# Attention followed by a mixture of experts: expert weights in quarters between the loads, q and k loaded pair by pair

## The chip, the core and the metric

The kernel runs on one core of a Trainium2 chip. The metric is the device time in microseconds of one execution; before the change it was 235.57 us, the median of three runs (233.94 to 238.21).

The engines are named as the profile names them: PE (TensorE, matrix products), DVE (VectorE), ACT (ScalarE), POOL (GpSimd), SP (SyncE, which only issues transfers here). Each runs its own instruction list strictly in order and waits on semaphores for the others. Transfers are issued by SP, ACT or POOL and are carried by 16 DMA engines that all of them share.

## The reference

```python
scores = scale * np.matmul(q, k.transpose(0, 1, 3, 2))    # (4, 8, 768, 768), head_dim 64
# retrieval heads 0, 2 and 6 see all earlier positions; the five streaming heads see the
# first 4 positions and a window of 64
mask = np.where(retr[0, :, 0, 0, None, None], full_mask, stream_mask)
a = softmax(np.where(mask, scores, -1e9));  attn = np.matmul(a, v)
x = attn.transpose(0, 2, 1, 3).reshape(3072, 512)
xc = x[x @ w_skip > 0];  logits = xc @ w_gate             # (512, 8)
e_idx = np.argmax(logits, axis=1);  gate_w = softmax(logits)[e_idx]
for e in range(8):
    h = np.maximum(xc[e_idx == e] @ w1[e], 0.0)           # (512, 1024)
    y[e_idx == e] = gate_w * (h @ w2[e])                  # (1024, 512)
out = x;  out[x @ w_skip > 0] = xc + y
```

So: attention for 4 x 8 heads of 768 tokens, then for the tokens with a positive skip score one expert of eight. The eight experts have two weight matrices each, 2 MB a matrix in fp32.

## The kernel before, in words

**Attention** goes over 16 pairs of heads (pair i: batch i // 4, heads 2(i % 4) and the next one). For each pair POOL casts q, k and v to fp16 (lines 659 and 665), PE transposes them (684, 695), ACT and DVE copy the transposes out of PSUM (`out_q` 712, `out_k` 722 with 729 and 730 for the sliding-window keys `kx`), PE forms the scores with their masks (818, 830), ACT takes the exponentials (840), PE weighs the values (881), and DVE divides (900, 907) and writes the pair's part of x (917). Three pairs in four have one retrieval head and one streaming head, the fourth has two streaming heads. For streaming heads POOL copies a part of the values (765, 767).

**Loads.** q, k and v of batch 0 come in parts, those of batches 1 to 3 as whole batches of 1.5 MB (`load`, 610 to 620), into five buffers that later also hold weights. For batch 0 a partition holds six tokens that follow each other, so a head's run is 1,536 bytes; for v and for the later batches a partition holds every 128th token, and a run is 256 bytes. SP issues them in order, together with the finished x of each batch (`x_out`, 926), which goes to `out`.

**Weights.** There are 16 halves (an expert's w1 or w2, 2 MB read, cast to 1 MB of fp16 on the way), numbered W0 to W15. POOL issues them (452), each at a place in its list tied to a cast. W0 to W10 stand in the attention part; W11 and W12 stand ahead of the gathers, W13 to W15 among and behind them.

**Routing** (1023 to 1057, then `fin`, 1122 to 1125): DVE and PE turn the gate logits into `idx`, 16 lists of 128 token rows, two lists for each expert.

**Experts.** POOL gathers the 16 lists of rows from `out` (1154), which must wait until all of x has been written there. For each list DVE casts (1178), PE transposes (1187), DVE copies out (1198). PE forms h for an expert (1207), ACT takes the relu (1218), PE forms y (1228), DVE adds gate times y to the rows (1235), and POOL scatters them back to `out` (1164). W0 and W1 belong to expert 0, W14 and W15 to expert 7.

**What sets the order.** Class `Plan` holds every step with an engine, an assumed duration, what it depends on and a priority. `lay` walks through time: it takes the engine that can start soonest and lets it do, of the steps that are ready there, the one with the lowest key. A transfer (`dma`) is two steps: the issue on an engine, and the transfer itself on a modelled queue "Q". `write` then emits the instructions in the order that came out. The order is fixed when the program is built: on the chip only semaphores decide when a step starts. There are two plans, one for attention with routing, one for the experts.

Of the kernel before, what the change touches and what calls it, by code (L numbers as in the profile page):

```python
# [52 lines left out]
class Plan:  # L53
# [8 lines left out]
    def op(self, name, eng, dur, fn, deps=(), key=0.0, lat=None, take=None):  # L62

        o = dict(name=name, eng=eng, dur=dur, fn=fn, deps=list(deps), key=key,
                 lat=self.LAT if lat is None else lat, take=take,
                 seq=len(self.ops))
        self.ops.append(o)
        self.by[name] = o
        return name

    def dma(self, name, eng, issue, kbytes, fn, deps=(), key=0.0, queue="Q",
            rate=370.0, lat=1.9):
        self.op((name, "go"), eng, issue, fn, deps, key)
        self.op(name, queue, kbytes / rate, None, [(name, "go")], len(self.ops),
                lat=lat)

    def lay(self, rings):
# [9 lines left out]
        ready, free, n = {}, {}, 0  # L87
# [5 lines left out]
        def at(o):  # L93
            if o["take"]:
                s = slots[o["take"][0]]
                if not s:
                    return None
                return max(when[o["name"]], min(s))
            return when[o["name"]]

        while n < len(self.ops):
# [21 lines left out]
            for u in users.get(o["name"], ()):  # L123
# [4 lines left out]
                if not need[u]:  # L128
                    ready.setdefault(v["eng"], []).append(v)
        return sorted(self.ops, key=lambda o: (o["start"], o["seq"]))  # L130

    def write(self, **rings):
        for o in self.lay(rings):
            if o["fn"] is not None:
                o["fn"]()

# [242 lines left out]
def kernel(  # L379
# [60 lines left out]
    NPRE = 7  # L440
    wts = {}

    def wtile(n, pool):
        e, half = divmod(n, 2)
        wts[e, half] = pool.tile([P, DS * F], FP16, name=f"w{half + 1}_{e}")
# [4 lines left out]
    def load_half(n):  # L450
        e, half = divmod(n, 2)
        nc.gpsimd.dma_start(out=wts[e, half], in_=(w1r, w2r)[half][e])

    ld_pool = ctx.enter_context(tc.tile_pool(name="ld", bufs=1))

    def slab(shape, dt, name):
        return ld_pool.tile(shape, dt, tag="big", bufs=5, name=name)

    def load_slab(n):
        def go():  # L460
            wts[divmod(n, 2)] = slab([P, DS * F], FP16, f"ws{n}")
            load_half(n)
        return go

    with tc.tile_pool(name="qk", bufs=1) as qk_pool, \
# [103 lines left out]
        dma("wgl", "ACT", 0.9, 60, l_wg, key=-90)  # L569
# [38 lines left out]
        big = {}  # L608

        def load(w, b, h0, h1, eng):  # L610
            def go():
                if h0 == 0:
                    big[w, b] = slab([P, H * NQB, D], FP32, w + "f")
                t = big[w, b][:, h0 * NQB:h1 * NQB]
                if b == 0 and w != "v":
                    eng.dma_start(
                        out=t.rearrange("p (h n) d -> p h (n d)", n=NQB),
                        in_=rows6[w][b, :, h0:h1])
                else:
                    eng.dma_start(out=t, in_=rows1[w][b, :, h0 * NQB:h1 * NQB])  # L620
            return go

        sp = iter(range(1000))
        where = {}
        order = [("q", 0, 0), ("k", 0, 0), ("v", 0, 0), ("q", 0, 1), ("k", 0, 1),
                 ("v", 0, 1), ("q", 0, 2), ("k", 0, 2), ("q", 0, 3), ("k", 0, 3)]
        order += [(w, b, 0) for b in range(1, B) for w in "qkv"]
        slabs = []
        for w, b, n in order:
            hs = (0, H) if b else (2 * n, 2 * n + 2)  # L630
            if (w, b, n) == ("v", 0, 1):
                hs = (2, H)
            for i in range(4 * b + hs[0] // 2, 4 * b + hs[1] // 2):
                where[w, i] = ("ld", w, b, n)
            old = None
            if n == 0:
                slabs.append((w, b))
                if len(slabs) > 5:
                    w2, b2 = slabs[-6]
                    old = ("C" + w2, 4 * b2 + 3)  # L640
            on_act = (w, b, n) == ("k", 0, 0)
            dma(("ld", w, b, n), "ACT" if on_act else "SP", 0.45,
                197 * (hs[1] - hs[0]) * (1.25 if w == "v" and not n + b else 1.06),
                load(w, b, *hs, nc.scalar if on_act else nc.sync),
                [old] + ([("ld", "q", 2, 0)] if w + str(b) == "k2" else []),
                -95 if on_act else next(sp))


        def fp32_of(w, i):
            h0 = 2 * (i % 4)  # L650
            return big[w, i // 4][:, h0 * NQB:(h0 + 2) * NQB].rearrange(
# [18 lines left out]
        for i in range(NPR):  # L670
            for w in "qk":
                op(("C" + w, i), "DVE" if i == 0 and w == "q" else "POOL", 0.87,
                   cast(i, w), [where[w, i], ("T" + w, i - 2)],
                   10 * (i - 2) + (1 if w == "q" else 2))
            op(("Cv", i), "POOL", 0.9, cast_v(i),
               [where["v", i], ("PV", i - 3, 1), ("Vx", i - 3), "vones"],
# [24 lines left out]
        def in_order(i, to, t):  # L701

            if i < 4:
                return (to.rearrange("d (p n) -> d p n", n=NQB),
                        t.rearrange("d n p -> d p n"))
# [639 lines left out]
```

## Time and profile before

| | us |
|---|---|
| median of three runs (233.94 to 238.21) | 235.57 |
| the execution that was profiled | 236.37 |
| its span, first to last instruction | 234.8 |
| attention and routing, to the last of `idx` and its gates | 0 to 134.84 |
| from there to the first gather | 134.84 to 151.91 |
| first product of an expert to the last | 159.18 to 221.73 |
| from there to the end of the span | 13.1 |

The profile is of one execution. A row of the view by line gives engine, operation, tiles, the shape, the count, the busy time, the mean of one in ns, and the idle time of the engine ahead of them with what ended it. The view by stretches gives the busy time of each engine in a stretch, then the clock of TensorE that was granted (1.00 is full), the busy share of the 16 DMA engines, and the GB/s they moved. "Busy" of an engine leaves out its waits; an idle engine costs time only where another waits for it.

### The profile page before, as it was taken

What the parts mean: (1) busy time and instruction counts of PE and PEld (TensorE: products, weight loads), DVE (VectorE), ACT (ScalarE), POOL (GpSimd) and SP (SyncE); (2) the same over time, 40 slices, a digit from 0 to 9 for tenths busy, and PEclk for the clock granted to TensorE, in tenths of its full rate; (3) what the DMA queues carried; (4) which work ended last, traced back from release to release, by engine and by line L of the source; (5) the groups of instructions that cost most, each with busy time, mean ns of one, the idle gap of its engine ahead of it and who ended that gap; (6) DMA issues with size and microseconds to landing.
All of it is one profiled execution on the core that took longest, in us unless ns stands there. A gap on an engine that the chain in (4) does not pass through costs nothing. (4 is left out here: it accounts for less than half of the span.)

```text
span 234.8 us, 4538 instructions
## 1 busy us (share of the span) xinstructions
PE 156.6 (67%) x1817; PEld 122.4 (52%) x1832; DVE 114.8 (49%) x305; ACT 98.3 (42%) x119; POOL 103.5 (44%) x158
## 2 busy tenths in 40 slices
PE   0597877893588953988872400019889999999700
PEld 0375666773477742877751300018756887667300
DVE  6576584752355732369999900035318645312400
ACT  2167465884077760688565900003143442234000
POOL 7639347900939207963361000177874233122510
PEclk9999799999589996799998555557999999999985
DMA  6999999998999999999999999236499931101100
GB/s 178 341 345 275 260 299 296 254 283 216 305 368 298 229 245 290 250 194 185 259 252 242 227 245 262 52 86 183 91 201 229 211 143 46 46 11 51 48 25 1
DMA packets 29517, 47.09 MB, mean 201 GB/s; under 512 B 4644, under 2 KB 23972, under 8 KB 27442
## 3 DMA queue, kind: packets, MB, share of 16 engines
q0 software_dynamic: 4864, 21.55, 42.4%
q1 hardware_dynamic: 23296, 24.77, 33.6%
q10 hardware_dynamic: 1330, 0.41, 0.7%
q8 instruction: 16, 0.26, 0.4%
q14 instruction: 11, 0.09, 0.1%
HBM read 56.64 MB, written 10.49 MB: 286 GB/s over the span
## 5 line engine op out<-in xcount | busy, mean ns | idle before, releaser
L840 ACT ACTIVATE at<-pst 128x1024 f16<-128x1024 f32 (+1 forms) x60 | 58.2, 1007 | 42.0 <-PE pst L830 41.5
L1218 ACT ACTIVATE ht<-hps 128x512 f16<-128x512 f32 x32 | 19.1, 597 | 61.7 <-PE hps L1207 52.9
L830 PE MATMUL pst<-qT,k 128*128 128x128 f16 (+2 forms) x308 | 38.0, 251 | 5.9 <-ACT qT L712 3.3
L830 PEld LDWEIGHTS <-k 128*128 128x128 f16 x308 | 26.1, 105 | 16.5 <-issue 8.1
L1164 POOL DMA_INDIRECT out_dram<-xg,idx x16 | 16.1, 1003 | 32.4 <-DVE xg L1235 29.9
L722 DVE COPY k<-tps 64x768 f16<-64x768 f16 x32 | 20.9, 654 | 16.0 <-PE tps L684 15.7
L881 PEld LDWEIGHTS <-at 128*128 128x128 f16 x472 | 19.2, 100 | 15.9 <-issue 12.0
L659 POOL CAST k<-kf 128x768 f16<-128x768 f32 x16 | 13.2, 825 | 30.5 <-DMA kf<-in_k_dram 29.7
L1154 POOL DMA_INDIRECT xg<-out_dram,idx x16 | 16.9, 1055 | 16.7 <-DMA out_dram<-x 12.1
L881 PE MATMUL opsa<-va,at 128*128 128x74 f16 x392 | 21.4, 199 | 3.5 <-DVE x L917 3.5
L1207 PE MATMUL hps<-xT,w 128*128 128x256 f16 x192 | 23.4, 281 | 0.2 <-issue 0.2
L1187 PE MATMUL xtp<-ident,x 128*128 128x128 f16 x64 | 6.4, 241 | 24.9 <-DVE x L1178 24.3
L1207 PEld LDWEIGHTS <-w 128*128 128x128 f16 x192 | 21.9, 145 | 1.5 <-issue 0.4
L1235 DVE SCALAR_TENSOR_TENSOR xg<-yps,gsl,xg 128x512 f32<-128x512 f32 x16 | 11.9, 749 | 18.3 <-PE yps L1228 17.9
L1178 DVE CAST x<-xg 128x512 f16<-128x512 f32 x16 | 9.5, 626 | 23.2 <-DMA xg<-out_dram,idx 23.2
L1228 PEld LDWEIGHTS <-ht 128*128 128x128 f16 x128 | 12.3, 98 | 14.0 <-issue 0.5
L1187 PEld LDWEIGHTS <-x 128*128 128x128 f16 x64 | 4.7, 107 | 26.1 <-DVE x L1178 25.1
L1228 PE MATMUL yps<-w,ht 128*128 128x512 f16 x80 | 18.1, 379 | 0.4 <-issue 0.4
L818 PE MATMUL pst<-smask,identb 128*128 128x512 bf16 (+3 forms) x49 | 16.9, 358 | 0.0
L665 POOL CAST va<-vf 128x768 f16<-128x768 f32 x16 | 13.1, 825 | 8.1 <-DMA vf<-in_v_dram 6.9
L881 PE MATMUL opsa<-vx,at 128*128 128x74 f16 x80 | 8.8, 207 | 11.7 <-POOL vx L767 11.7
L765 POOL COPY vx<-va 64x296 f16<-64x296 f16 x20 | 9.9, 493 | 14.7 <-DVE va L754 5.7
(120 smaller groups left out, 263.6 us busy)
## 6 DMA issues: line engine op xcount, KB each, us to landing
w<-in_moe_w_dram POOLq DMA_DIRECT2D x11, 1024.0 KB
ws<-in_moe_w_dram POOLq DMA_DIRECT2D x5, 1024.0 KB
out_dram<-x SPq DMA_DIRECT2D x3, 1536.0 KB, 18.6
qf<-in_q_dram SPq DMA_DIRECT2D x4, 384.0 KB, 5.3
kf<-in_k_dram SPq DMA_DIRECT2D x3, 384.0 KB, 5.0
out_dram<-x SPq DMA_DIRECT2D x1, 768.0 KB, 23.0
out_dram<-x SPq DMA_DIRECT2D x2, 384.0 KB, 20.4
kf<-in_k_dram ACTq DMA_DIRECT2D x1, 384.0 KB, 4.7
```

The costliest lines, as they stand in the source:

```text
L659: e.tensor_copy(t, fp32_of(w, i).rearrange("p h n d -> p n h d"))
L665: nc.gpsimd.tensor_copy(vab[i % 3][:, :, GX:GX + 2 * D].rearrange("p n (h d) -> p h n d", h=2), fp32_of("v", i))
L722: nc.vector.tensor_copy(to, ti)
L818: nc.tensor.matmul(pst[:, c0 - c * CH:c0 - c * CH + m].rearrange("p (n c) -> p n c", c=P), identb, mv, start=(n == 0), stop=(n == last))
L830: nc.tensor.matmul(pst[:, c0 - c * CH:c0 - c * CH + m * P], lt, qTs[i][:, qb * P:(qb + m) * P], start=(n == 0), stop=(n == last))
L840: nc.scalar.activation(ats[i][:, c * CH:c * CH + cn], psts[i, c][:, :cn], ACT.Exp, scale=SCALE)
L881: nc.tensor.matmul(opss[i][:, hi, qb * VA:(qb + 1) * VA], ats[i][:, b0 + c:b0 + c + P], vb, start=(n == 0), stop=(n == len(todo) - 1))
L1154: h = nc.gpsimd.indirect_dma_start(out=xgs[:, t], out_offset=None, in_=out[:, :], in_offset=bass.IndirectOffsetOnAxis(ap=idx[:, t:t + 1], ...
L1164: h = nc.gpsimd.indirect_dma_start(out=out[:, :], out_offset=bass.IndirectOffsetOnAxis(ap=idx[:, t:t + 1], axis=0), in_=xgs[:, t], in_offs ...
L1207: nc.tensor.matmul(hps[:, fi, :], w1[:, s, 2 * f2 + fi], xTs[e][:, s, :], start=(fi == 0 and s == 0), stop=(fi == 1 and s == DS - 1))
L1218: nc.scalar.activation(hts[e][:, 2 * f2:2 * f2 + 2], hpss[e, f2], ACT.Relu)
L1228: nc.tensor.matmul(yps, hts[e][:, j, s2 * P:(s2 + 1) * P], w2[:, j], start=(j == 0), stop=(j == FS - 1))
```

## The change

It changes how the weights are cut and where their issues stand, how q and k are loaded, and a few steps of routing:

- Weights go in quarters (half of a W, 1 MB read). In the plan each quarter has `fill`: its issue may not start before the modelled queue has less than that many us left to do (0.5 in attention, 2.0 for the experts). Quarters have the last priority in attention. Those that the plan would start after `idx` are left to the second plan, where they alternate with the gathers.
- q and k are loaded pair by pair, all with six tokens to a partition, into four buffers each (`load_qk`); v stays in batches, in two buffers. `out_q` and `out_k` then have the reordering copy for all pairs that batch 0 had before, and the `kx` copies read the copied k instead of PSUM.
- x of a batch is written in two transfers instead of one.
- Routing: the token lists' table `R` is made by POOL instead of DVE; the one-hot table `L` in 4 operations over six columns each instead of 24 over one.
- A drain stands on POOL behind the twelfth scatter.
- The modelled durations are adjusted.

```diff
-    def lay(self, rings):
+    def lay(self, rings, busy=0.0):
...
         def at(o):
+            t = when[o["name"]]
+            if o["fill"] is not None:
+                more = sum(x["dur"] for x in ready.get("Q", ()))
+                t = max(t, free["Q"] + more - o["fill"])
...
-        nc.gpsimd.dma_start(out=wts[e, half], in_=(w1r, w2r)[half][e])
+        c = slice(u * DS * F // 2, (u + 1) * DS * F // 2)
+        def go():
+            nc.gpsimd.dma_start(out=wts[e, half][:, c],
+                                in_=(w1r, w2r)[half][e][:, c])
...
+        def load_qk(i, w, eng):
+            def go():
+                b, hs = heads(i)
+                t = ldq_pool.tile([P, 2, NQB, D], FP32, tag=w + "f", bufs=NLD,
+                                  name=w + "f")
+                eng.dma_start(out=t.rearrange("p h n d -> p h (n d)"),
+                              in_=rows6[w][b, :, hs[0]:hs[0] + 2])
...
-            if i < 4:
-                return (to.rearrange("d (p n) -> d p n", n=NQB),
-                        t.rearrange("d n p -> d p n"))
-            return to, t.rearrange("d n p -> d (n p)")
+            return (to.rearrange("d (p n) -> d p n", n=NQB),
+                    t.rearrange("d n p -> d p n"))
...
-            dma(("W", n), "POOL", 0.9, 2097,
-                load_slab(n) if n >= NPRE else lambda n=n: load_half(n),
-                [after] + free, 10 * after[1] - 15.5, rate=400)
+            dma(name, "POOL", 0.58, 2.65, load_quarter(*name[1:]),
+                [("Cv", 1), (fill[x - 1], "go") if x else None], 500 + x,
+                first=True, fill=0.5)
...
-                "R": lambda: v.tensor_tensor(
+                "R": lambda: nc.gpsimd.tensor_tensor(
...
-                fns["L", m] = lambda m=m: v.tensor_scalar(
-                    T["L"][:, c0 + m], iota16, h128[:, m:m + 1],
-                    rank[:, m:m + 1], ALU.add, ALU.is_equal)
+                fns["L", m] = lambda m=m: v.tensor_tensor(
+                    T["L"][:, c0 + m:c0 + m + NQB], ...
...
+            dma(name, "POOL", 0.58, 2.65, load_quarter(*name[1:]),
+                [(fill[x - 1], "go") if x else None], -50 + x, first=True,
+                fill=2.0)
+        for t in range(NT):
+            dma(("G", t), "POOL", 1.25, 0.4, gather(t), [("z", t // 2 * 2)],
+                -100 + t if t < 4 else -48 + 0.7 * t, first=True)
...
+        op("drain", "POOL", 2.0, lambda: nc.gpsimd.drain(), [("S", 11)], 11.5)
```

How the order moves. POOL, the start of the program, after the change; `ident` is the identity for the transposes, `w_3_95` holds W7, expert 3's w2:

```order
L516 MEMSET ident 128x128
L474 DMA w_3_95<-in_moe_w_dram 128x2048
L517 ISA
L517 AFFINE_SELECT ident<-ident 128x128
L523 CAST identb<-ident 128x128
```

Before, no transfer stood there, and W0 was the first weight, behind the casts of the third pair. Now one quarter of W7 (the second plan's first) comes out at the very start, and W0's first quarter stands behind the casts of k of the eighth pair. Up to the gathers there are 16 quarters, W0 to W7, instead of 13 halves.

POOL around the end of attention, before (`ws` and `w` are weights, `vx` the copied values of streaming heads, `xg` the gathered rows):

```order
L452 DMA ws_2064<-in_moe_w_dram 128x4096
L765 COPY vx_131<-va_127 64x296
L767 COPY vx_131<-va_127 64x296
L452 DMA ws_2150<-in_moe_w_dram 128x4096
L452 DMA w_5_2305<-in_moe_w_dram 128x4096
L452 DMA w_6_2306<-in_moe_w_dram 128x4096
L1154 DMA xg<-out_dram,idx 128x512 x12
L452 DMA w_6_2307<-in_moe_w_dram 128x4096
L1154 DMA xg<-out_dram,idx 128x512 x4
```

and after the change:

```order
L779 COPY vx_136<-va_132 64x296
L781 COPY vx_136<-va_132 64x296
L1065 TENSOR_TENSOR tables<-r_oht,val 128x18x64
L474 DMA w_3_94<-in_moe_w_dram 128x2048 x2
L474 DMA w_3_95<-in_moe_w_dram 128x2048
L1065 TENSOR_TENSOR tables<-r_oht,val 128x6x64
L1174 DMA xg<-out_dram,idx 128x512 x4
L474 DMA w_4_96<-in_moe_w_dram 128x2048
L1174 DMA xg<-out_dram,idx 128x512
L474 DMA w_4_96<-in_moe_w_dram 128x2048
L1174 DMA xg<-out_dram,idx 128x512 x3
L474 DMA w_4_2346<-in_moe_w_dram 128x2048
```

Before, W10, W11 and W12 stood between the last copy of values and the first gather, each a half. Now three quarters stand there (W6 whole, the first of W7) beside the two steps that make `R`, and W8 to W10 alternate with the gathers. W11 to W15 follow in quarters among the first ten scatters.

## Rows read from the trace of the kernel before

**Rows 1.** The page: span; DMA's busy tenths in 40 slices of 5.87 us.

```profile
span 234.8 us, 4538 instructions
DMA  6999999998999999999999999236499931101100
```

**Rows 2.** By stretches: busy (x count) PE, PEld, DVE, ACT, POOL; clock, DMA share, GB/s.

```profile
50.00:100.00 50.00, 34.81 (x493) 28.95 (x497) 22.59 (x60) 25.90 (x30) 24.79 (x41) 0.86 1.00 274
100.00:135.00 35.00, 23.84 (x393) 19.52 (x395) 31.44 (x104) 25.31 (x29) 12.62 (x22) 0.90 1.03 226
135.00:152.00 17.00, 0.00 (x0) 0.00 (x0) 0.00 (x0) 0.00 (x0) 0.62 (x2) 0.50 0.81 193
159.00:222.00 63.00, 61.04 (x442) 44.62 (x440) 25.72 (x54) 19.06 (x32) 28.10 (x29) 0.98 0.45 113
```

**Rows 3.** Waits: who waited for whom, us in total, times, the longest.

```profile
POOL k L659 <- DMA kf<-in_k_dram: 29.7, 4, 11.7
```

**Rows 4.** POOL in order of time: start, us, the instruction, idle before it.

```profile
46.04 0.53 POOL L452 DMA_DIRECT2D w<-in_moe_w_dram  x1
...
58.28 0.83 POOL L659 CAST k<-kf 128x768 f16<-128x768 f32 x1 [11.72 <-DMA kf<-in_k_dram]
```

**Rows 5.** DVE in order of time: x of pairs 4, 6, 8, 10, 12, 14.

```profile
50.37 0.95 DVE L917 TENSOR_TENSOR x<-opsa,recs 128x768 f32<-128x768 f32 x1
...
69.12 0.94 DVE L917 TENSOR_TENSOR x<-opsa,recs 128x768 f32<-128x768 f32 x1
...
80.88 0.94 DVE L917 TENSOR_TENSOR x<-opsa,recs 128x768 f32<-128x768 f32 x1
...
99.98 0.94 DVE L917 TENSOR_TENSOR x<-opsa,recs 128x768 f32<-128x768 f32 x1
...
112.11 0.95 DVE L917 TENSOR_TENSOR x<-opsa,recs 128x768 f32<-128x768 f32 x1
...
124.50 0.94 DVE L917 TENSOR_TENSOR x<-opsa,recs 128x768 f32<-128x768 f32 x1
```

**Rows 6.** DMA queues, whole span: packets, MB written, share of 16 engines' time.

```profile
q0 software_dynamic: 4864, 21.55, 42.4%
q1 hardware_dynamic: 23296, 24.77, 33.6%
```

**Rows 7.** The same from 100 to 135 us (q0 POOL's, q1 SP's).

```profile
q0 software_dynamic: 829, 6.04, 87.3%
q1 hardware_dynamic: 1022, 1.81, 14.6%
```

**Rows 8.** In order of time: routing's end, first gather, its cast, expert products.

```profile
134.66 0.18 DVE L1125 TENSOR_TENSOR gsl<-msb 128x16 f32<-128x16 f32 x1
...
151.91 1.10 POOL L1154 DMA_INDIRECT xg<-out_dram,idx  x1 [12.08 <-DMA out_dram<-x]
155.31 1.15 DVE L1178 CAST x<-xg 128x512 f16<-128x512 f32 x2 [20.47 <-DMA xg<-out_dram,idx]
159.18 1.91 PE L1207 MATMUL hps<-xT,w 128*128 128x256 f16 x8
218.11 3.62 PE L1228 MATMUL yps<-ws,ht 128*128 128x512 f16 x16
```

**Rows 9.** By tile x: its transfers to out, from issue to landing.

```profile
DMA to landing us min/median/max: 11.8/20.8/31.5
```

**Rows 10.** DVE: one line's durations in ns; then groups by line.

```profile
L722 DVE COPY k<-tps x32: 538/560/961, 10.7 to 115.0; 64x768 f16<-64x768 f16 x32
L729 DVE COPY kx<-k 64x256 f16<-64x256 f16 x5 | 2.4, 487 | 0.2
L729 DVE COPY kx<-tps 64x256 f16<-64x256 f16 x15 | 4.3, 284 | 0.0
L1057 DVE TENSOR_SCALAR tables<-iota,r_h,r_rank 128x128 f16<-128x128 f16 x24 | 6.1, 325 | 0.0
```

**Rows 11.** SP's waits at the program's end.

```profile
SPq L1340 <- PEq L1340: 6.7, 2, 6.2
```

More of the change, by code (lines that the diff above doesn't have):

```diff
@@ L69, in op, with dma @@
         return name
[L71 to L74, printed above, removed]
+    def dma(self, name, eng, issue, took, fn, deps=(), key=0.0, first=False,
+            lat=1.9, fill=None):
+        self.op((name, "go"), eng, issue, fn, deps, key, fill=fill)
+        self.op(name, "Q", took, None, [(name, "go")], 0 if first else 1,
                 lat=lat)
-    def lay(self, rings):
+    def lay(self, rings, busy=0.0):
         users, need, gives = {}, {}, {}
@@ L86, in lay @@
         when = {o["name"]: 0.0 for o in self.ops}
[L87 removed]
+        ready, free, n = {}, {"Q": busy}, 0
         slots = {r: [0.0] * m for r, m in rings.items()}
@@ L129, in lay, with write @@
                     ready.setdefault(v["eng"], []).append(v)
+        self.free = free
         return sorted(self.ops, key=lambda o: (o["start"], o["seq"]))
-    def write(self, **rings):
-        for o in self.lay(rings):
-            if o["fn"] is not None:
+    def write(self, busy=0.0, until=None, **rings):
+        ops = self.lay(rings, busy)
+        end = 1e9
+        if until is not None:
+            end = max(o["start"] + o["dur"] for o in ops if o["name"] in until)
+        left = []
+        for o in ops:
+            if o["fill"] is not None and o["start"] > end:
+                left.append(o["name"][0])
+            elif o["fn"] is not None:
                 o["fn"]()
+        took = sum(self.by[n]["dur"] for n in left)
+        return left, max(0.0, self.free["Q"] - took - end)
 def gate_ops(nc, pool, C, glog, nch, gate_out, oh_out):
@@ L611, in go, with load_v @@
+        def load_v(b, h0, h1):
             def go():
                 if h0 == 0:
[L613 to L620, printed above, removed]
+                    v32[b] = slab([P, H * NQB, D], FP32, "vf")
+                c = slice(h0 * NQB, h1 * NQB)
+                nc.sync.dma_start(out=v32[b][:, c], in_=rows1["v"][b][:, c])
@@ L621, in load @@
             return go
+        NLD = 4
         sp = iter(range(1000))
[L624 to L646, printed above, removed]
@@ new lines @@
+        for i in range(NPR):
+            for w in "qk":
+                act = i == 0 and w == "k"
+                dma(("ld", w, i), "ACT" if act else "SP", 0.45, 1.07,
+                    load_qk(i, w, nc.scalar if act else nc.sync),
+                    [("C" + w, i - NLD)], -95 if act else next(sp))
+            if i == 0:
+                dma(("ldv", 0), "SP", 0.45, 1.8, load_v(0, 0, 2), (), next(sp))
+            elif i == 1:
+                dma(("ldv", 0, 1), "SP", 0.45, 3.4, load_v(0, 2, H), (), next(sp))
+            elif i % 4 == 3 and i // 4 + 1 < B:
+                b = i // 4 + 1
+                dma(("ldv", b), "SP", 0.45, 4.5, load_v(b, 0, H),
+                    [("Cv", 4 * b - 5)], next(sp))
@@ L671 @@
             for w in "qk":
-                op(("C" + w, i), "DVE" if i == 0 and w == "q" else "POOL", 0.87,
-                   cast(i, w), [where[w, i], ("T" + w, i - 2)],
+                op(("C" + w, i), "DVE" if i == 0 and w == "q" else "POOL", 0.83,
+                   cast(i, w), [("ld", w, i), ("T" + w, i - 2)],
                    10 * (i - 2) + (1 if w == "q" else 2))
             op(("Cv", i), "POOL", 0.9, cast_v(i),
-               [where["v", i], ("PV", i - 3, 1), ("Vx", i - 3), "vones"],
+               [("ldv", 0, 1) if 0 < i < 4 else ("ldv", i // 4), ("PV", i - 3, 1), ("Vx", i - 3), "vones"],
                10 * (i - 2) + 4)
@@ L1240 @@
             op(("z", t), "ACT", 0.95, zero(t, t + 2), key=t - 100)
[L1241 removed]
[4 rows of a table removed]
[L1246 to L1253 removed]
+        fill = left + [("W", n, u) for n in range(NPRE, 2 * E) for u in range(2)]
+        for x, name in enumerate(fill):
+            dma(name, "POOL", 0.58, 2.65, load_quarter(*name[1:]),
[4 more added lines that the diff above has]
+                -100 + t if t < 4 else -48 + 0.7 * t, first=True)
         for t in range(NT):
```

162 lines of the change are left out of this document (81 added, 81 removed), and 4 rows, old and new, of the table gorder.

## The prediction

> **What bounds the kernel now.** I read four views. First the page and the view by stretches: the DMA engines are busy nine tenths or more in nearly every slice up to about 147 us [rows 1], and from 100 to 135 us their share is 1.03 while no engine is at its limit but DVE, with 31.44 of 35 us [rows 2]. So attention is short of transfers, with DVE close behind. From 159 to 222 us the picture turns round: PE works 61.04 of 63 us, and the DMA engines 0.45 of it [rows 2]. Between the two lie 17 us in which nothing computes [rows 2]. The transfers are too many before the gathers and too few after them.
>
> Second, the queues. POOL's queue writes 6.04 MB from 100 to 135 us and takes 87.3% of the engines for it [rows 7], that is 30.6 us, or 5.06 us for a MB. A half of weights writes 1.049 MB: 5.3 us. A quarter is 2.65 us. Over the span POOL's queue takes 42.4% [rows 6], 99.6 us; 16 halves are 84.8 of them, and the 32 gathers and scatters share the other 14.8, 0.46 us each. SP's queue takes 33.6% [rows 6], 78.9 us. Before the gathers stand 13 halves: 68.9 + 78.9 = 147.8 us. That is the time at which the DMA engines come to rest, and it is why the first gather goes out at 151.91 [rows 8].
>
> Third, the waits: POOL waited 29.7 us for k, in four waits [rows 3]. The two longest come after a weight was put into the queue: a half goes out at 46.04, and the next cast of k starts at 58.28 after 11.72 us of idling [rows 4]; the other long wait is of the same kind, 31 us later. While both queues had work, SP's got 14.6% [rows 7]: loads that share the engines with a half of weights crawl.
>
> Fourth, the order of time at the seam. Routing is done at 134.84, W12 goes out behind it, the gathers wait 12.08 us for x to be written and start at 151.91, and the first expert product comes 7.27 us later, at 159.18 [rows 8]. Writes of x took 11.8 us at best and 31.5 us at worst from issue to landing [rows 9]. The last product ends at 221.73 [rows 8], and 13.1 us follow to the end of the span.
>
> **The change, part by part.** The sum is against the profiled execution: span 234.8, 236.37 us with what lies around it, 0.8 above the median of 235.57.
>
> *Loads by pairs, weights later.* Weights now give the loads a long start: the first quarter behind a cast comes after k of pair 7, where a half came behind the third pair. The starved stretches should go. From pair 4 to 6 the x of a pair moved by 18.75 us, from 8 to 10 by 19.10, and from 12 to 14, with routing beside it but without a wait for k, by 12.39 [rows 5]. If both fall to that, 6.4 + 6.7 = 13.1 us are saved. I take **-13.1**; the bounds are 0 (something else holds the pairs to the old pace) and -29.7, all of the waiting for k [rows 3], which the quickest such step in the rows gives no ground for.
>
> *The quarter at the start.* The order shows one quarter of W7 as the first transfer that POOL issues, beside the loads of pair 0. It can hold them up by nothing, or by its whole 2.65 us. The first loads wait for nothing else, so I take **+2**.
>
> *The reordering copies.* L722 takes 0.54 to 0.56 us for a plain copy, and 0.96 for the reordered one of batch 0 [rows 10]. 24 copies change over: 24 x 0.4 = 9.6 us more of DVE. The `kx` copies read SBUF instead of PSUM: 487 ns as a mean of the five that did so already, 284 for the others [rows 10], so 15 x 0.2 = 3.0 us. Cover: DVE is idle for 27.4 of the 50 us from 50 to 100 and 3.6 of the 35 behind them [rows 2]; but each copy stands ahead of its pair's scores. Between 0 and 12.6 I take **+2**, near 0 for the first of these rows.
>
> *Routing.* 24 steps of `L` cost 6.1 us, the last six among them after the last pair [rows 10]. In their place stand 4 operations over 768 elements; x (L917), also a tensor_tensor over 768, takes 0.95 [rows 5]. At the end of routing that is one of 0.95 for six of 0.25, and `R` goes to POOL beside it: **-0.5**, bounds -1.5 and +1 (POOL's version is not in the trace).
>
> *The seam.* Up to the gathers the DMA engines now have 16 quarters, 42.4 us, and 78.9 us of SP's: 121.3 us, about as long as attention now lasts. So the last x no longer stands behind two halves. After the last x is issued it needs a share of the engines with what is left of three quarters, and its own landing. The gather's way from issue to cast, with the engines free, took 3.4 us (151.91 to 155.31) [rows 8], and that is the floor of such a way; the best x landing, 11.8 [rows 9], is the ceiling. I take 5.1 in place of 17.1: **-12**, bounds -13.7 and -5.3.
>
> *The experts.* PE's work is the same, 62.5 us from 159.18 to 221.73 [rows 8]. W8 to W15 now come in this part: 16 quarters, 42.4 us, and 14.8 for gathers and scatters, 57.2 us of transfers in some 70. A gather behind a quarter in POOL's queue lands up to 2.65 us later, and the transposes of the third expert stand early in PE's list. Two such delays are 5.3 us, none is 0: **+2**.
>
> *The end.* An earlier drain can shorten only the last wait, of which SP saw 6.7 us in two pieces [rows 11]. Between 0 and -6.2 I take **-1.5**, near zero, since no row shows how the wait depends on earlier drains. The early drain stands where POOL waits for the last experts anyway.
>
> Sum: -13.1 + 2 + 2 - 0.5 - 12 + 2 - 1.5 = **-21.1**. That is 236.37 - 21.1 = 215.3 for an execution like the profiled one, and 0.8 less for a median: **214.5 us**.
>
> **A rule that speaks against it.** The row shows halves that follow each other at 5.06 us a MB with the engines' share at 1.03 [rows 2, 7], so the landing of one lies beside the transfer of the next. The Trainium skill (DMA: Bandwidth & Descriptors, "Measured (HBM→SBUF, 128 partitions, SWDGE, issued from GpSimd)") says to batch transfers to 1 MiB or more for three quarters of the peak, and its section on the anatomy of one DMA puts a fixed 2 us on each. By that, quarters are the wrong way: 16 more transfers of 2 us would add an estimated 32 us of queue time if nothing overlapped. No run here has a quarter yet, so the trace neither agrees nor differs.
>
> **The rivals.**
>
> *A. Attention does not get shorter.* DVE is the bound behind the loads: 31.44 of 35 us near the end [rows 2], and it gains up to 12.6 us. Then routing ends at 134.8 as now, the first three terms come to 0, and -0.5 - 12 + 2 - 1.5 = -12 is left: 223.6 us. Against it: from 50 to 100 us alone DVE is idle for more than twice what it gains. Chance 0.17.
>
> *B. Each quarter pays for its own landing.* Place: the experts' weights. The rule of the Trainium skill above is of this kind. The first gather took 3.4 us from issue to cast, of which 0.46 is data, so 2.9 us is fixed. If quarters paid that one after another, each would take 5.55 us, and 16 of them with the 14.8 us of the other transfers 104 us, where PE needs 62.5 + 7.3. The kernel would end about 34 us later than I forecast: 249 us. It decides from some 5.1 us a quarter on; there the experts' transfers come to 96 us, 26 over what I forecast, and the kernel is 2% slower than now. Against it: in the rows above several halves are under way at once. Chance 0.05.
>
> *C. The quarters don't fill gaps.* The queue is modelled and the order fixed, so the chip may run it at other times. Then the three quarters ahead of the gathers meet the last x, and the seam stays at 17.1 us. The sum is -9.1: 226.5 us for a median. For it: the list puts them there. Against it: they are 8 us of transfers where 13 halves were due. Chance 0.07.
>
> *D. Better.* Copies and the early quarter cost nothing, the seam falls to its floor, and the drain gives 4 us: -13.1 - 0.5 - 13.7 - 4 = -31.3, 204.3 us. Chance 0.04.
>
> **The numbers.** The forecast has a chance of 0.63, and 0.04 is left for no change by some cause that I don't see. The range goes from 204 (D) to 225, over A. Outside lie C, B, the 0.04 for no change, and 0.04 of the forecast and D at the lower end: 0.2 in all. A measurement of this kernel tells 2% from nothing, that is below 230.9 or above 240.3. Forecast, A, C and D are faster: 0.91. Same 0.04, slower 0.05.
>
> **What would show it.** Right: POOL's wait for k falls from 29.7 us to a few; x of pairs 4 to 6 and 8 to 10 moves by 12 to 13 us; the last gate is done near 124 us; the first gather follows within 6 us; DMA's share in the experts' part rises from 0.45 to 0.75 or more, with PE still busy nearly throughout. Wrong: DVE near 100% in attention (A); PE waiting for weights in the experts' part (B); a first gather more than 12 us behind routing (C). If POOL's first casts of k and v come more than 3 us later than now, the early quarter was underrated.

## The result

The changed kernel takes **204.02 us** (median of four runs, 202.74 to 206.17) where the kernel before took 234.75 (four runs beside it): a ratio of 0.869, interval 0.857 to 0.882, so faster by 30.7 us. A second series, made later, gave 203.99 (six runs) and 0.866 (0.858 to 0.874). The ratios leave out executions that took over 1.5% more than the fastest of their kernel. The forecast was 214.5 with a range of 204 to 225: the sign was right, the size was short by ten, and the time lies at the very edge of the range. The rows of after are those of a profiled execution of the second series: 204.64 us, span 203.0.

The page of after: span, clock and DMA in 40 slices of 5.08 us, and the two large queues (packets, MB, share of the engines).

```profile
span 203.0 us, 4596 instructions
PEclk9999999999999999999999755579999999999985
DMA  5999999899999999999999972599999999995010
q0 software_dynamic: 7168, 21.55, 51.7%
q1 hardware_dynamic: 20560, 24.78, 36.3%
```

Read these lines against [rows 1, 6]. The time of the two queues together has not changed: 76.0% of 234.8 is 178.4 us before, 88.0% of 203.0 is 178.6 after. (POOL's queue rose from 99.6 to 104.9, SP's fell from 78.9 to 73.7.) What shrank is the rest of the span, from 56.4 to 24.4 us: 32.0, as much as the span lost. **The change moved transfers into time in which the DMA engines had rested.** In the first half they were busy before as after.

By stretches, with the columns of [rows 2]:

```profile
50.00:100.00 50.00, 43.39 (x704) 36.39 (x708) 42.93 (x91) 37.59 (x43) 34.19 (x57) 1.00 1.02 278
120.00:131.00 11.00, 1.15 (x9) 0.70 (x9) 2.76 (x9) 2.35 (x3) 5.74 (x6) 0.50 0.32 89
131.00:192.00 61.00, 60.90 (x442) 45.01 (x442) 25.98 (x54) 19.12 (x32) 35.08 (x41) 0.97 0.93 201
```

In attention PE does 43.39 us of work in 50 instead of 34.81, with a granted clock of 1.00 instead of 0.86, and DVE 42.93 instead of 22.59; in the experts' part DMA's share is 0.93 instead of 0.45, and PE is still busy throughout. POOL's wait for k [rows 3] is now

```profile
POOL k L677 <- DMA kf<-in_k_dram: 0.8, 2, 0.5
```

DVE's x of pairs 0, 4, 6, 8, 10, 12 and 14, which answer to [rows 5]; then, as in [rows 8], the last gate, the first gather, its cast, the first and the last product, and the last scatter:

```profile
28.88 0.94 DVE L931 TENSOR_TENSOR x<-opsa,recs 128x768 f32<-128x768 f32 x1
...
50.49 0.95 DVE L931 TENSOR_TENSOR x<-opsa,recs 128x768 f32<-128x768 f32 x1
...
62.38 0.95 DVE L931 TENSOR_TENSOR x<-opsa,recs 128x768 f32<-128x768 f32 x1
...
73.43 0.95 DVE L931 TENSOR_TENSOR x<-opsa,recs 128x768 f32<-128x768 f32 x1
...
85.31 0.95 DVE L931 TENSOR_TENSOR x<-opsa,recs 128x768 f32<-128x768 f32 x1
...
97.45 0.95 DVE L931 TENSOR_TENSOR x<-opsa,recs 128x768 f32<-128x768 f32 x1
...
107.64 0.94 DVE L931 TENSOR_TENSOR x<-opsa,recs 128x768 f32<-128x768 f32 x1
...
120.36 0.18 DVE L1144 TENSOR_TENSOR gsl<-msb 128x16 f32<-128x16 f32 x1
...
124.04 1.14 POOL L1174 DMA_INDIRECT xg<-out_dram,idx  x1 [5.64 <-issue]
...
127.48 1.16 DVE L1198 CAST x<-xg 128x512 f16<-128x512 f32 x2 [6.95 <-DMA xg<-out_dram,idx]
...
131.39 1.91 PE L1227 MATMUL hps<-xT,w 128*128 128x256 f16 x8
...
184.83 7.07 PE L1248 MATMUL yps<-w,ht 128*128 128x512 f16 x32
...
194.52 0.99 POOL L1184 DMA_INDIRECT out_dram<-xg,idx  x1 [0.30 <-issue]
```

From these rows and [rows 5, 8], the span's 31.8 us by stretch:

| stretch | before | after | moved | forecast |
|---|---|---|---|---|
| start to last gate | 134.66 | 120.36 | -14.3 | -9.6 |
| last gate to first gather | 17.25 | 3.68 | -13.6 | -12 |
| first gather to last product's end | 69.82 | 67.86 | -2.0 | +2 |
| from there to the end of the span | 13.1 | 11.1 | -2.0 | -1.5 |

A second profile of the same order of instructions (drain_s7, below) moves by -13.0, -13.7, -1.3 and -4.0. So the first two rows are known to about 1 us and the last two only to about 2.

### The profile page after: what moved, and what is told of

Same layout as the page of the kernel before. It is cut to its first block, busy times and chain, and to the rows that moved or that the text cites. A ratio compares the mean times of both kernels' runs of the same rounds, so it can differ in the third digit from the quotient of the medians.

```text
span 204.2 us, 4608 instructions
## 1 busy us (share of the span) xinstructions
PE 151.1 (74%) x1832; PEld 118.4 (58%) x1832; DVE 125.9 (62%) x285; ACT 98.0 (48%) x119; POOL 116.8 (57%) x176
## 5 line engine op out<-in xcount | busy, mean ns | idle before, releaser
L844 PE MATMUL pst<-qT,k 128*128 128x128 f16 (+2 forms) x308 | 35.6, 241 | 6.5 <-ACT qT L728 3.8
L738 DVE COPY k<-tps 64x768 f16<-64x768 f16 x32 | 30.5, 954 | 10.3 <-PE tps L702 10.1
L1227 PE MATMUL hps<-xT,w 128*128 128x256 f16 x256 | 31.8, 284 | 0.0
L1227 PEld LDWEIGHTS <-w 128*128 128x128 f16 x256 | 29.5, 146 | 2.0
L1248 PE MATMUL yps<-w,ht 128*128 128x512 f16 x128 | 28.9, 379 | 0.0
L832 PE MATMUL pst<-smask,identb 128*128 128x512 bf16 (+2 forms) x64 | 22.3, 359 | 0.4 <-ACT at L854 0.2
L895 PE MATMUL opsa<-va,at 128*128 128x74 f16 x392 | 19.7, 196 | 0.3 <-ACT at L854 0.3
L1248 PEld LDWEIGHTS <-ht 128*128 128x128 f16 x128 | 12.3, 98 | 13.2
L474 POOL DMA_DIRECT2D w<-in_moe_w_dram x32 | 18.6, 583 | 0.4 <-issue 0.4
L779 POOL COPY vx<-va 64x296 f16<-64x296 f16 x20 | 8.7, 437 | 14.6 <-DVE va L768 10.4
L728 ACT COPY qT<-tps 128x768 f16<-128x768 f16 x16 | 12.8, 799 | 6.9 <-PE tps L702 6.9
L677 POOL CAST k<-kf 128x768 f16<-128x768 f32 x16 | 13.2, 826 | 3.6 <-PE tps L702 3.0
L931 DVE TENSOR_TENSOR x<-opsa,recs 128x768 f32<-128x768 f32 x16 | 15.1, 946 | 0.0
```

What stands on the lines that cost most here:

```text
L474: nc.gpsimd.dma_start(out=wts[e, half][:, c], in_=(w1r, w2r)[half][e][:, c])
L738: nc.vector.tensor_copy(to, ti)
L832: nc.tensor.matmul(pst[:, c0 - c * CH:c0 - c * CH + m].rearrange("p (n c) -> p n c", c=P), identb, mv, start=(n == 0), stop=(n == last))
L844: nc.tensor.matmul(pst[:, c0 - c * CH:c0 - c * CH + m * P], lt, qTs[i][:, qb * P:(qb + m) * P], start=(n == 0), stop=(n == last))
L895: nc.tensor.matmul(opss[i][:, hi, qb * VA:(qb + 1) * VA], ats[i][:, b0 + c:b0 + c + P], vb, start=(n == 0), stop=(n == len(todo) - 1))
L931: nc.vector.tensor_mul(xsb[i // 4][:, :, h0 * D:(h0 + 2) * D].rearrange("p n (h d) -> p h n d", h=2), summed(i, GX, 512 - GX, D), recs[:, ...
```

## The experiments

All are small edits of the changed kernel, but for one of the kernel before. Times are medians; ratios are to the kernel before on the same chip. The runs come from several chips, on which the median of the kernel before goes from 232.97 to 237.15 us, so a difference of one or two us between chips says little. One chip ran no_hoist, b_late, rows1 and halves, one q_tail, weights_last, no_drain and drain_s7, one plain and v1, and one v2 and the second series of the changed kernel. Rows and steps are of one profile each.

**no_hoist.** The left-over quarter gets something to wait for:

```diff
-                [(fill[x - 1], "go") if x else None], -50 + x, first=True,
-                fill=2.0)
+                [(fill[x - 1], "go") if x else (("G", 3), "go")], -50 + x,
+                first=True, fill=2.0)
```

> The changed kernel, but the left-over quarter of W7 is issued behind the fourth gather instead of as POOL's first transfer. Theory 1 (the early quarter holds up the gate's weights, and with them the first copies on DVE, so the whole of attention stands 4.7 us later): x of pair 0 starts near 25 us instead of 29.6, everything behind it moves along, 199 to 200.5 us against 204.0. Theory 2 (the DMA engines are full until about 112 us, so the quarter's 2.65 us of transfer only change places and attention ends where it does now): 202 to 204.

Measured: 208.06 us (0.894, 0.885 to 0.903), 4 us *slower*. Both theories miss. The first is right about attention: DVE takes the gate's weights (`wgb`) at 9.58 instead of 12.28 us, x of pair 0 comes at 25.50 instead of 28.88, and the experts' first weights go into PE at 128.1 instead of 131.3. DVE in no_hoist and then in the changed kernel:

```profile
9.58 0.63 DVE L576 CAST wgb<-wg 64x36 f16<-64x36 f32 x1 [3.57 <-DMA wg<-in_moe_w_skip_dram]
```

```profile
12.28 0.43 DVE L576 CAST wgb<-wg 64x36 f16<-64x36 f32 x1 [6.44 <-DMA wg<-in_moe_w_skip_dram]
```

It is wrong that the rest moves along. PE in order of time in no_hoist, near the end:

```profile
182.80 5.17 PE L1227 MATMUL hps<-xT,w 128*128 128x256 f16 x30 [2.66 <-DMA w<-in_moe_w_dram]
187.80 7.07 PE L1248 MATMUL yps<-w,ht 128*128 128x512 f16 x32
```

PE now waits for weights, 3.7 us in all, and the experts take 66.7 us from their first weights on instead of 60.6. The other 2.4 us are PE's own work, 62.9 us instead of 60.5, at a mean granted clock of 0.94 instead of 0.97: from 183.8 to 187.0 us, behind the waits, it was 0.50 (the lower of its two levels). A quarter less ahead of the gathers is a quarter more in a stretch whose DMA engines are full (their share from 128 to 180 us is 1.01). The early quarter costs attention 3 us (last gate at 120.36 instead of 117.37) and more than pays for itself at the end.

**q_tail.** As no_hoist, and `fill=None if name == ("W", 7, 1) else 0.5` in the first plan.

> The changed kernel with the same 16 quarters ahead of the gathers, but the sixteenth behind the fifteenth, near 107 us, and not at the program's start. Theory 1 (the transfers are the bound from end to end, and the seam leaves them idle, so a quarter there costs nothing and saves the experts 2.65 us): x of pair 0 near 25.5 us as without the early quarter, seam at most 1.5 us longer than its 3.5, no wait of PE for weights over 1 us, 199 to 202 us against 204.0 and 208.1. Theory 2 (a quarter beside the last x holds it up by its own length): the first gather comes 6 us or more behind the last gate, 203 to 206 us.

Measured: 206.02 us (203.39 to 206.45; 0.878, 0.869 to 0.887). As theory 1 has it, PE keeps its pace, 61.7 us for the experts with one wait of 1.2 us for weights; in the direction of theory 2, but less than its 6 us, the first gather comes late, 5.36 us behind the last gate instead of 3.68. Four quarters now go out in a row ahead of the last x, and part of the fourth is paid there. Another 2.0 us of this profile say nothing about the quarter: attention loses them against no_hoist between pairs 0 and 4, where both kernels have the same order.

**weights_last.** As no_hoist, and `("Cv", 1)` becomes `("Cv", 11)` in the dependencies of the quarters.

> As the run without the early quarter, but no weights at all are issued until pair 13 is being cast (near 80 us), 12 quarters are ahead of the gathers and 20 behind. Read for the pace of pairs 4 to 10, which stand there without any weights beside their loads. Theory 1 (the engines hold the pairs, the quarters fill gaps): x of pair 10 stays within 1 us of the 82.3 it has with weights beside it. Theory 2 (transfers hold attention): it comes 3 us or more earlier. The end by the theory that transfers are the bound behind the seam: three quarters more in the experts' part than in the run without the early quarter, 8 us later, 214 to 217; if PE were the bound there, 207 to 210.

Measured: 213.93 us (two runs; 0.918). Pairs 4 to 10 take 34.80 us (48.88 to 83.68) without weights beside them, and in the changed kernel 34.82 with them. The same stretch without and with weights (no_hoist):

```profile
50.00:82.00 32.00, 28.35 (x476) 23.91 (x474) 26.04 (x51) 23.45 (x26) 21.50 (x35) 1.00 0.87 249
```

```profile
50.00:82.00 32.00, 27.79 (x470) 23.44 (x466) 27.46 (x54) 23.89 (x27) 22.65 (x37) 1.00 1.06 318
```

DMA's share falls from 1.06 to 0.87 and the pairs come no sooner: the engines hold attention now, and the quarters do fill gaps. (When pair 4 comes is not compared: x of pair 0 lies between 24.8 and 27.4 us in the eight kernels without the early quarter, and between 28.9 and 30.1 in the four profiles with it.) Behind the seam PE waits 9.7 us for weights. From the first product to the last the experts take 75.0 us instead of no_hoist's 66.6: the 8 us that three quarters were to cost. The time is only 5.9 us longer, since the end behind the last product is 3.3 shorter (8.7 instead of 12.0).

**b_late.** The kernel before, with eight halves of weights ahead of the gathers instead of thirteen (the diff leaves out the list of the gathers, where W8 to W10 now stand among them):

```diff
-        for n, after in enumerate((
-                ("Cv", 2), ("Cv", 4), ("Cv", 6), ("Cv", 8), ("Cv", 10),
-                ("Cv", 12), ("Cv", 13), ("Cv", 14), ("Cv", 15), ("Vx", 14),
-                ("Vx", 15))):
+        for n, after in enumerate((("Cv", 6), ("Cv", 8), ("Cv", 9), ("Cv", 10), ("Cv", 11), ("Cv", 12), ("Cv", 13), ("Cv", 14))):
...
-                    (), -100 + n, rate=400)
+                    [(("G", 3), "go")], -100 + n, rate=400)
```

> The kernel before with one thing moved: eight halves of weights instead of thirteen are issued ahead of the gathers, the first at pair 6 instead of pair 2, the other eight behind the gathers. Loads, pieces and copies are those of before. Theory 1 (when the weights are issued decides): the gathers start within 6 us of the last gate, -11, and POOL's wait for k falls from 29.7 us to 10 or less, -5 to -13: 211 to 219 us against 234.75. Theory 2 (it needs loads by pairs and quarters too): the seam shrinks, but a load of a whole batch is starved by any half beside it, so attention keeps its pace: 222 to 227. Theory 3 (the placement does nothing by itself): 231 or more.

Measured: 219.37 us (0.944, 0.934 to 0.953), between theories 1 and 2. Its last gate, first gather and POOL's wait for k:

```profile
132.38 0.18 DVE L1122 TENSOR_TENSOR gsl<-msb 128x16 f32<-128x16 f32 x1
...
136.02 1.10 POOL L1153 DMA_INDIRECT xg<-out_dram,idx  x1 [15.12 <-issue]
```

```profile
POOL k L659 <- DMA kf<-in_k_dram: 19.1, 4, 15.2
```

The seam falls to 3.64 us: **the placement alone gives the whole term of the seam**, and 17.2 of the span's 31.8 us. Attention moves by 2.3 us only; one load of a whole batch still waits 15.2 us beside halves.

**rows1.** As no_hoist, with q and k of pairs 4 to 15 in the old layout:

```diff
+                if b:
+                    eng.dma_start(
+                        out=t.rearrange("p h n d -> p (h n) d"),
+                        in_=rows1[w][b, :, hs[0] * NQB:(hs[0] + 2) * NQB])
...
+            if i >= 4:
+                return to, t.rearrange("d n p -> d (n p)")
```

> As the run without the early quarter, but q and k of pairs 4 to 15 are loaded with 256-byte runs, as before the change, still by pairs, and their copies out of PSUM are the plain ones again. Theory 1 (run length is worth its 5 us of transfer time in a stretch where the DMA engines are full): SP's queue takes 78 us or more instead of 73.5, attention ends 3 to 6 us later, 202 to 206 us. Theory 2 (DVE has room, so the reordering copies cost nothing, but transfers are hidden as well): within 1.5 us of the run without the early quarter. Theory 3 (the copies of 0.95 us are on the path): 1.5 to 6 us faster than that run.

Measured: 221.28 us (0.952, 0.939 to 0.964), 13.2 slower than no_hoist. Theory 1 has the direction and is far too small. SP's queue, rows1 and then no_hoist:

```profile
q1 hardware_dynamic: 51280, 24.78, 40.6%
```

```profile
q1 hardware_dynamic: 20560, 24.78, 35.7%
```

The same bytes take 89.0 us (of 219.2) instead of 73.9 (of 206.9): 15.1 us more transfers, and POOL waits 34.4 us for q and k again. The 13.2 us are net of what the plain copies of 12 pairs give back (for all pairs 4.9 us, by the run plain), so the layout is likely worth more than that. Loads by pairs in the old layout win nothing: b_late, with whole batches, takes 219.37. No run has whole batches in the new layout, so what the pairs add to it is not shown. The Trainium skill (DMA: Bandwidth & Descriptors, "Specifications") wants 512 B or more for a transfer at line rate; for loads by pairs the trace agrees, with 30,720 more packets and 15.1 us.

**halves.** As no_hoist, but the second quarter's place issues the whole half (`out=wts[e, half]`) and the first's nothing.

> As the run without the early quarter, but each half of weights is one transfer, put out where its second quarter stood. Theory 1 (what counts is how many bytes stand in the queue and when, not the size of a piece): within 1.5 us of the run with quarters, POOL's wait for k stays below 3 us. Theory 2 (halves squeeze the loads as before the change): POOL waits 8 us or more for k, 3 to 8 us slower than with quarters.

Measured: 210.66 us (0.907, 0.898 to 0.915), 2.6 slower than no_hoist, between the two theories. POOL waits 1.4 us for k, so nothing is squeezed as before. x of pair 0 is 1.5 us later, which is within the scatter given above, and the experts take 1.2 us longer. POOL's queue takes 49.3% of 209.0, 103.0 us, and with quarters 49.9% of 206.9, 103.2.

**plain.** As no_hoist; `in_order` returns `to, t.rearrange("d n p -> d (n p)")`.

> As the run without the early quarter, but the copies of q and k out of PSUM leave the tokens of q and k in the order in which they come (token 6p+n stays in column 128n+p), so that the masks fall on other tokens; everything that is timed is the same otherwise. Theory 1 (the reordering copies are on the path of attention now that loads do not hold it): pairs 4 to 6 take 10 us instead of 11.9, attention ends 6 us or more earlier, near 104 instead of 109.7; of that the end keeps 2 us or less, since the weights still come at the pace of the transfers. Theory 2 (they lie beside other work, the exponentials on ACT and the products hold the pairs): attention ends within 1.5 us of 109.7.

Measured: 203.16 us (two runs; 0.870, 0.864 to 0.875), 4.9 faster than no_hoist. The k copies by their group, plain and then in the changed kernel (count, us busy, mean ns):

```profile
L737 DVE COPY k<-tps 64x768 f16<-64x768 f16 x32 | 17.7, 554 | 12.8 <-PE tps L702 12.5
```

```profile
L738 DVE COPY k<-tps 64x768 f16<-64x768 f16 x32 | 30.5, 954 | 10.3 <-PE tps L702 10.1
```

ACT's copies of q take 800 ns either way, and the `kx` copies, which now read a plain k, take 1.6 us more. Of the 12.8 us that DVE saves on k, 4.2 were on the path: attention's last reciprocal comes at 105.50 instead of no_hoist's 109.70. Pairs 4 to 6 take 11.48 instead of 11.9, so neither theory has the size. And the end keeps all of it, against my expectation: the quarters' places are in POOL's list, so they come sooner with the pairs (the fifteenth goes out at 103.9 instead of 108.1 us), and the experts take 2.9 us less.

**no_drain.** The changed kernel without `op("drain", ...)`.

> The changed kernel without the early drain. Theory 1 (the drain takes 8 us of POOL and gives 3.6 us back at the last drain and 0.9 at the semaphores behind it, while it makes the last scatter 2 us late): the last scatter goes out within 0.4 us of its add, the last drain takes 4 us again, and the end comes 1.5 to 3 us later, 205.5 to 207. Theory 2 (the last drain waits for the last scatters alone): 202 us, 2 us faster, with a last drain of some 0.5 us as with the early one.

Measured: 210.36 us (0.901, 0.894 to 0.908): 5.2 slower than drain_s7 (below), which is the changed kernel on the same chip, and 6.3 slower than the first series; more than theory 1, and theory 2 has the wrong sign. Up to the first gather the profiles of no_drain and drain_s7 agree within 0.3 us; of the 6.8 us between their spans, 5.5 lie behind the last product (14.6 and 9.1). POOL's drains at the program's end (durations in ns: least, median, longest), before, without the early drain, and in the changed kernel (the profile of its first series, span 204.2):

```profile
L1340 POOLq DRAIN  x3: 50/103/4061, 229.9 to 234.5; - x3
```

```profile
L1357 POOLq DRAIN  x3: 46/103/5367, 203.4 to 209.3; - x3
```

```profile
L1358 POOLq DRAIN  x3: 46/103/445, 202.9 to 203.9; - x3
```

The last drain took 4.06 us behind 48 transfers issued by POOL, 5.37 behind 64, and 0.44 behind the 4 since the early one: an estimated 0.08 us for each transfer and 0.1, from these three. The quarters made it longer; the early drain pays that beforehand.

**drain_s7.** `[("S", 7)], 7.5` for the drain's place.

> The changed kernel with the early drain behind scatter 7 instead of 11. Theory 1 (a drain takes as long as what is in flight in front of it, weights among it, and POOL issues nothing in the meantime): it holds up the quarters that stand behind it, PE waits for weights, 205 us or more. Theory 2 (the drain costs the 2 us only where it stands, at the last scatters): the last four scatters follow their adds at once, and the end comes 2 us earlier, 202 us.

Measured: 205.13 us (0.877, 0.869 to 0.886). It tells nothing about the drain's place: the planner counts a scatter's transfer behind the weights, and the drain still came behind scatter 11. The order of instructions is that of the changed kernel, so the run stands for a repeat of it.

**v1.** Three edits on the changed kernel:

```diff
-            dma(name, "POOL", 0.58, 2.65, load_quarter(*name[1:]),
+            dma(name, "POOL", 0.58, 2.65 if x else 0.0, load_quarter(*name[1:]),
...
-                first=True, fill=0.5)
+                first=True, fill=0.5 if x else None)
...
-                [(fill[x - 1], "go") if x else None], -50 + x, first=True,
-                fill=2.0)
+                [(fill[x - 1], "go") if x else (("G", 1), "go")], -50 + x,
+                first=True, fill=2.0)
...
-                -100 + t if t < 4 else -48 + 0.7 * t, first=True)
+                -100 + t if t < 2 else -48 + 0.7 * t, first=True)
...
-        op("drain", "POOL", 2.0, lambda: nc.gpsimd.drain(), [("S", 11)], 11.5)
+        op("drain", "POOL", 2.0, lambda: nc.gpsimd.drain(),
+           [(("S", 9), "go"), (fill[-1], "go")], 9.5)
```

> The changed kernel with three edits: no quarter at the program's start, the first quarter of W0 goes out behind the cast of v of pair 1 instead; two gathers instead of four ahead of the first weights behind the seam; the early drain behind scatter 9 and the last weights. Theory 1 (16 quarters ahead of the gathers keep the experts fed, and a quarter among prefetched loads costs attention nothing, where the one at the start cost it 4 us): pair 0 near 25.5 us, last pair near 110, no wait of PE for weights over 1 us, the last scatter within 0.5 us of its add, span near 199, 198 to 201 us. Theory 2 (the transfers are full in attention, a quarter more there costs its 2.65 us wherever it stands): 201 to 204 us.

Measured: 202.65 us (0.869, 0.864 to 0.873). In its stretches theory 1 holds up to the end: pair 0 at 25.36, the experts in 61.4 us without a wait of PE for weights. The time is in the range of theory 2. The drain misses: issued with weights in flight it took 12.37 us, and the last scatter went out 2.5 us behind its add.

**v2 and after_again.** v1 with the drain behind scatter 11, and one more behind R: `op("drain0", "POOL", 1.5, lambda: nc.gpsimd.drain(), [("r", 1, "R")], 300)`; beside it the changed kernel as it is.

> As v1, but the early drain stands behind scatter 11 again, and a second one behind the last product of R, where POOL waits some 5 us for x. Theory 1 (a drain takes until what is in flight has landed, and then some 0.085 us for each transfer that POOL issued since the drain before: 5.37 us for 64 without an early drain, 4.06 for 48 in the kernel before, 0.44 for 4): the first ends before x has landed and moves nothing, the second takes 6 us or less instead of 8.0, the last scatter goes out within 1 us of its add instead of 2.2, span near 198.5, 199 to 201.5 us. Theory 2 (a drain has a length of its own of some 8 us): the first gather comes 2 us or more later, the scatters bunch as before, 203 us or more.

> The changed kernel as it is, for a comparison on the same chip: 203 to 205.5 us.

Measured: **v2 199.71 us** (six runs, 199.45 to 201.57; 0.849, 0.842 to 0.855), the changed kernel 203.99. v2 beats both kernels; every run of it is below every run of the changed kernel beside it (203.12 to 205.99). Its two drains:

```profile
L1147 POOLq DRAIN  x1: 4605/4605/4605, 116.1 to 116.1; - x1
```

```profile
L1322 POOLq DRAIN  x1: 6992/6992/6992, 180.6 to 180.6; - x1
```

The first ends at 120.7, ahead of the first gather at 122.42, which comes 3.5 us behind the last gate as without it. The second takes 7.0 us where 6 were expected, and the last scatter goes out 1.4 us behind its add: the direction of theory 1, not its whole size. Which of the edits gives the gain is not shown. Of the 3.6 us between the two profiles 1.5 lie ahead of the last gate and 1.9 behind the last product, where v2 takes 9.3 us, the changed kernel 11.1, and its repeat drain_s7, with one drain, 9.1.

## Why the prediction was right, and where it was short

The time lies in the range by 0.02 us, and that is luck: the second series lies 0.01 below it. The mechanism was right; most terms were mis-sized, as follows.

- **Starved stretches** (-13.1). Right in mechanism: POOL's wait for k is 0.8 us, and the two long steps shrank, 4 to 6 from 18.75 to 11.89 us, 8 to 10 from 19.10 to 11.88. Those two gave 14.1 us even with the slower copies in them. This is the term that was mis-sized most: the last gate comes 14.3 us sooner although the early quarter and the copies cost 3.0 and 4.2 by their runs and routing gives 0.2, which makes an estimated 21 us of it.
- **The quarter at the start** (+2). Too small: x of pair 0 comes 4.0 us later (24.92 to 28.88), and the last gate 3.0 us later than in no_hoist. The place was right, the way not: the gate's weights come late and DVE stands in front of them. That it costs time in all was wrong; moved behind the gathers it costs more. The sign that I had named for it, first casts over 3 us late, did not show: v's came at 9.86 instead of 7.31.
- **The copies** (+2). 4.2 by the run without the reordering (plain, against no_hoist); that the `kx` copies read SBUF is not in this, for no run changes it.
- **Routing** (-0.5). -0.2: 7.88 us from the last reciprocal to the last gate before, 7.67 after. No run changes it alone, and none that x is written in two transfers.
- **The seam** (-12). Right, at its floor: 3.68 us for 17.25; I had taken 5.1 for fear that the last x shares the engines. The kernel before with the weights moved (b_late, 3.64) shows that it is the placement.
- **The experts** (+2). Wrong in sign: -2.0, or -1.3 in the repeat. Gathers behind quarters delayed no product; the first product comes 7.35 us behind the first gather, as before (7.27), and PE, which before did 60.9 us of work in the 62.5 to the last product, does not idle at all (60.5 in 60.5). What bounds this part was missed: from 131 to 177 us the DMA engines' share is 1.03, there is no room, and one quarter more costs PE 3.7 us of waiting.
- **The end** (-1.5). -2.0, or -4.0 in the repeat, and not by one term: the early drain takes 4.9 us off the last one, which the quarters would have made 1.3 longer, and it makes the last scatter late: 1.8 us behind the end of its add, where it was 0.3.

Two things stand behind the size of the first term. It left out the third wait for k, 6.21 us, which falls between x of pair 0 and x of pair 4. POOL in the kernel before:

```profile
32.58 1.60 POOL L659 CAST k<-kf 128x768 f16<-128x768 f32 x2 [6.21 <-DMA kf<-in_k_dram]
```

From pair 0 to pair 4 the rows moved by 25.45 us before and by 21.61 after: 3.8 less, for which the forecast has nothing. (From 12 to 14 they moved by 2.2 less, but from 14 to the last gate by 2.6 more.) And the 12.39 us that I took for a step were too many. They are the slowest of the three steps in [rows 5] without a wait for k (11.76 from 6 to 8, 12.13 from 10 to 12), and in plain these two take 10.84 each. Why they are quicker there is open.

The sum also has no word on the clock. In each of the two long steps of before PE stood idle behind the wait for k (5.1 us up to 60.2, 5.6 us up to 91.1), and the granted clock was 0.50 from 59.5 to 66.2 us and from 90.3 to 96.9. After the change it is 1.00 from 50 to 100 us. So a part of what the waits cost came behind them; how large it is, no run shows.

One reading of the prediction was wrong. The 14.6% of SP's queue from 100 to 135 us [rows 7] is no share of loads: SP issued its last load at 74.9 us, and in that stretch only writes of x. During the wait of [rows 4], from 46.0 to 58.3 us, SP's queue had 46.2% and POOL's 50.7%. Loads beside a half were late, but they had about half of the engines and not a seventh.

Of the signs, the last gate came at 120.4 us instead of near 124, the two steps of x took just under 12 us, and the first gather, DMA's share and POOL's wait stand as forecast. Rival A fell (DVE has 42.93 of 50 us, and the pairs came sooner), and so did C. B fell too: POOL's queue took 103.2 us with quarters (no_hoist) and 103.0 with halves. Several were under way at once; three quarters went out at 110.0, 110.6 and 111.1 us, where one takes 2.65. B's rule, to batch transfers to 1 MiB or more, is one of the Trainium skill (DMA: Bandwidth & Descriptors, "Measured (HBM→SBUF, 128 partitions, SWDGE, issued from GpSimd)"); the prediction's estimate by it, with the fixed 2 us of the page's section on the anatomy of one DMA, was 32 us for sixteen more transfers. The trace differs: it was 0.2 us. (A quarter reads 1 MB and writes half of it, so by the bytes read it is at the rule's edge.) D named the right time, 204.3, for reasons of which two are false: neither the copies nor the early quarter were free.

## What to carry to other kernels

Add up the queues' time and subtract it from the span: what is left is the most that a change of order alone can win; here it was 56.4 us, and the change won 32.0. Before taking a transfer out of an early stretch, look where it lands; in a stretch that is full it costs more than it cost before. And when stalls go, count all of them: a third wait, left out of the sum, was half as long as each of the two that stood in it.

## What was not expected of the hardware

- A drain of POOL at the program's end, with none of its transfers in flight, takes time by the number that POOL issued since the drain before: 0.44 us for 4, 0.61 for 6, 4.06 for 48, 5.37 for 64. One that is issued with transfers in flight also waits for them: in v1 it took 12.37 us and ended 2.9 us behind the last packet of POOL's queue. One early drain brings the time from the last product to the end of the span from 14.6 us (no_drain) to between 9.1 and 11.1; that a second one does more is not shown (9.3 in v2).
- Loads whose rows are 256 bytes long in memory are not alike: by whole batches SP's queue moved all its bytes in 23,296 packets and 78.9 us [rows 6], by pairs in 51,280 and 89.0. Why the packets differ stays open.
